# A new order table for a hand-ordered attention and mixer program, and alpha2 of the first batch as a scale at the PSUM copies

## The chip, the cores and the metric

The kernel runs on one core of a Trainium2 chip. The metric is device time in microseconds (us), lower is better; the time of a kernel is the median of its runs. A profile shows one execution: TensorE (PE; its weight loads are PEld), VectorE (DVE), ScalarE (ACT), GpSimd (POOL), SyncE (SP) and the DMA queues.

## The reference

Block-sparse attention over 4 batches of 8 heads with 768 positions of 64 elements, followed by a mixer MLP over the 512 columns of all heads together:

```python
scores = q @ k.T / sqrt(64)                # per batch and head, 768 x 768
mask: |block_i - block_j| <= 1, first and last block row and column, 3 drawn blocks per block row (32 wide)
attn = softmax(where(mask, scores, -1e9))
x = attn @ v                               # heads side by side: [4, 768, 512]
a1 = alpha1 * x + beta1
u  = x + lam * (w_tok @ a1)                # over the 768 positions
a2 = alpha2 * u + beta2
out = u + lam * (relu(a2 @ w_ch1) @ w_ch2) # 512 -> 2048 -> 512
```

## The kernel before

All work of the four batches lies in one program without loops at run time. A string of words, `ORDER` (some 2,000 of them), names every step in the order in which it is emitted; a loop (L848 to L852) reads it and calls the step of each word. `pin_order` (L121) then fixes on each engine the order in which its instructions were emitted, and `bank_order` (L138) makes uses of one PSUM bank follow each other. So the string is the schedule: on each engine a step that waits holds all later steps of that engine. A word is a kind and a number, for some with a PSUM bank or an engine behind a colon (`d` is DVE, `a` is ACT). Two heads are a pair; pairs are numbered 0 to 15 over the batches, four to a batch, and the numbers in words count pairs, score units (nine to a pair), thirds, halves or tiles.

- `lq`, `lk`, `lv` load a pair with a cast, by POOL's DMA queue (L403), into a pool of six buffers. From pair 7 on the load is held until a flag (`F`, a tiny write on DVE, L420) by a copy on POOL (L401). `cq`, `ck`, `cv` cast or copy the loaded tile on (`copy`, L385 ACT, L387 DVE), and with that the buffer comes free. `tq`, `tk` transpose q and k by DMA from SP (L554); the first pairs go through PE instead (`H`, `hq`, `hk`).
- `q` are the scores of one unit on PE (L585 for the first five pairs, where the mask is part of the product; L595, on 64 rows, for the others), `e` the exponential on ACT (L606), `m` the mask as a minimum on DVE (L613, from pair 5 on), `p` and `r` the values on PE (L619), `n` and `nt` the division by the sums on DVE (L653, L654).
- `a`, `b` form alpha1 * x + beta1 on DVE (L691, L697), `k` is the token mix on PE (L721; needs `b`), `x` adds it to x on DVE (L730). `u` makes the bfloat16 copy `ub` of a half of a pair's columns, and `U` transposes it into `uT`: by PE into a PSUM bank for the four pairs of batch 0 (L769), with `v` as the copy from PSUM, and by a DMA transpose on SP for pairs 4 to 15 (L763).
- `f` is one 128 x 384 tile of the first channel product on PE (L787, four matmuls over the four pairs of the batch, the last of them on the pair transposed last), `g` the relu on ACT or DVE (L801, L803), `h` a quarter of an output tile of the second product on PE (L821, four matmuls), `o` the final addition on DVE (L831), `s` the write of the output on SP (L840).
- alpha2: for batch 0 `u` multiplies by `a2_bc`, a 128 x 512 tile that a broadcast load (`lc3`, 256 KB) fills. After batch 0's `f` words the eight `P` words scale `w1b` itself by `a2T` (alpha2 as 128 x 4, load `lc5`; L750 ACT, L752 DVE), and later batches use plain casts in `u`.
- `lt`, `lw`, `lx`, `lc` load weights and parameters, `z` are matmuls without a use, at the start.

Of the kernel before, what the change touches and what calls it, by code (L numbers as in the profile page):

```python
# [47 lines left out]
q1:2 e1 lv0 lk1 lq1 q0:3 lt1 cq0 hm0 z352:0 H1:2 lq2 lk2 q2:0 q3:2 e0 hq1:d hk1:d e3 q4:1 cv0:d lv1
lt0 q6:3 p0:4 e4 p1 z480:5 z128:5 q8:1 ck1:d e2 lt2 lq3 z480:5 z352:5 q5:0 p2 e6 cq1:d lk3 p3 e5 lc1
p4 q7:3 H2:5 n0 e7 r4:0 r5 r6 lc0 lc2 hk2:d H3:1 hq2:d e8 W3:4 hk3:d q9:3 lc5 r7 hq3:d q12:1 cq2:d  # L50
e9 ck2:d w3:d lv2 lq4 W2:1 r8 e12 q11:3 cv1:d H4:5 lk4 e11 n1 q10:1 p9:4 hk4:d hq4:d H5:0 e10 q16:3
hq5:d W0:5 e16 q15:1 lc3 p10 w0:d hk5:d w2:d F21 e15 lc4 lk5 p11 q13:3 W1:0 e13 q14:1 W5:5 e14 p12
# [10 lines left out]
f30:4 g9:d g30:d S5 f28:2 tk5 g28:a g29:a n8 N0 f7:3 f24:7 f0:4 f4:1 f27:2 g7:d f22:5 ck7:a f26:0
f5:3 g6:d g4:d g24:d g0:a F26 F27 g5:a F28 lv8 S1 S2 f25:1 lq9 f2:4 f23:3 f16:6 g25:d g22:a lk9 g2:d
ck8:d g23:a g26:a f3:5 O0 g16:d r40:1 g3:d lv6 r41 g27:a cq8:a tk8 r42 tk6 r43 q47:3 S0 q48:1 e47
r44 f19:0 n9 e48 f1:5 g19:d q53:3 g1:a q51:0 q52:1 f21:4 a4 e51 b4 g21:a e52 f20:5 f18:0 g20:d k9:1
f17:5 m51 m47 e53 g18:a tq6 cv7:a x9 m53 m52 g17:a k8:3 tq8 q50:0 tk7 e50 q45:3 q49:2 x8 p51:2 p52
m48 p53 e49 e45 cq9:a P7:a nt17 h0:1 F29 m49 m50 h1 F30 cv6:a F31 h2 p48:6 p49 p50 h3 lv9 lq10 lk10
nt16 q46:3 q59:2 F32 q58:1 e46 ck9:d h8:0 o0 m45 lv10 s0 tq9 m46 e59 u9:a e58 F33 m59 F34 lq11 h9
p45:6 u8:a p46 p47 h4:1 nt15 tq7 q62:1 q56:3 q61:2 a5 h10 h5 h11 e62 F35 F36 m62 m58 e56 e61 m56  # L70
q57:2 q55:1 q60:3 cv8:d lk11 o2 cq11:d b5 e57 h6 lv11 e60 ck10:d m57 lq12 P4:d h7 e55 p57:5 p58 o1
p59 U4 q70:3 q54:1 q69:0 cq10:a F37 nt19 s1 m60 e70 h20:4 lk12 tk9 s2 m61 e54 e69 m70 k10:6 p60:5
m55 p61 p62 tk10 q64:0 q66:1 F38 x10 q76:3 nt20 m69 e64 e76 h21 k11:5 m54 e66 p54:6 ck12:d cq12:a
p55 p56 x11 nt18 F39 cv9:d lv12 h22 u11:a q67:3 q65:1 q68:0 e65 h23 h24:5 p69:2 lq13 a6 m64 F40 e68
u10:a lk13 b6 m66 F41 m68 k12:3 e67 ck11:a p70 q71:0 e71 q63:3 h25 m65 x12 o5 m67 lv13 p66:4 e63 m71
k13:1 m63 x13 p67 u13:a p71 tk11 p68 U5 nt23 nt22 p63:7 p64 u12:a P6:a p65 h26 nt21 F42 a7 b7 h27 U6
tq10 q78:1 q74:0 q72:3 e78 k14:4 o6 x14 e74 k15:5 x15 m78 u14:d u15:a e72 s5 h16:1 h17 P5:d m74 U7
P0:d ck13:d h18 lq14 cv10:d F43 q80:2 q75:1 q81:3 tq11 e75 lk14 m72 h19 e81 f46:0 f44:2 P1:a f47:3
# [5 lines left out]
g58:a e85 m89 g55:d a8 b8 m83 f53:5 f39:0 f32:4 f35:1 g53:a g39:a m82 g35:d g62:d g32:a f50:7 g50:d
f60:2 g60:a f57:3 m85 f61:4 g57:a q87:0 q93:3 g61:a q84:1 e84 k17:5 p81:4 e93 k16:2 e87 x17 m84
f63:6 x16 p84:3 m87 g63:a p82 p85 p86 nt28 p83 p87:5 nt27 q92:3 q98:0 q88:1 h36:4 tk12 s6 u17:d e92
m92 e88 e98 h37 h38 m88 s4 m98 p88 p89 h39 nt29 a9 b9 m91 o9 m93 q90:1 q94:3 q95:0 e95 h32:5 e94 e90
m90 m95 h33 h34 m94 q96:3 q100:0 q105:1 tq12 s9 e96 k18:4 h35 tq13 m96 p93:6 o8 x18 cv12:d p90:7
e100 e105 p94 p91 p92 q97:0 nt30 q110:1 q107:2 e97 p95 k19:7 nt31 e107 m97 p96:6 tk14 e110 x19
q103:0 q102:2 m107 u16:a p97 p98 u19:d nt32 u18:d e103 m105 a10 U8 h40:2 h41 tk13 U9 e102 m102 h42  # L90
q101:3 q104:0 p105:4 h43 e101 p102:3 b10 e104 m101 k21:5 m103 m104 p103 o10 q99:0 q106:3 ck15:a e99
s8 p104 h52:2 s10 e106 x21 m100 m99 k20:5 m106 p99:0 p100 nt34 p101 p106 p107 h48:3 m110 nt33 nt35
x20 h53 a11 q118:3 b11 q108:0 e118 q111:2 h49 e108 u20:a k22:6 u21:d k23:7 x22 U10 h50 cq15:d x23
e111 h54 h51 h55 q114:2 u22:a u23:d U11 tq14 o13 f75:0 f72:6 f74:7 f78:1 f73:2 e114 f67:5 tk15 g72:d
# [6 lines left out]
p115 g83:d m117 g91:a p124 f80:3 p116 g82:a cv15:d p125 nt38 p117:5 h64:4 g80:d nt41 p118 h65 a12
q133:3 q119:0 q122:1 e119 b12 cv14:d h66 e133 h67 m119 e122 p119 o16 h68:0 nt39 q121:3 q130:1 q120:2
m122 k25:1 h69 e120 m120 e121 k24:4 e130 m121 p120:7 x24 p121 p122 x25 h70 nt40 h71 a13 b13 q131:2
q128:3 q126:1 e131 e126 e128 u24:a k26:1 h88:4 x26 m131 o17 u25:d k27:5 q129:3 q136:1 m126 q140:0
x27 U12 h89 e129 h90 u27:d m129 s17 s16 m130 m128 e140 e136 h91 q127:0 q134:1 o22 e127 q132:3 p129:5
m133 p130 s22 p131 e134 m127 h84:0 nt43 p126:1 p127 p128 m134 q135:1 e132 q142:2 q138:3 e135 m132
nt42 h85 e142 e138 p132:2 m135 m136 p133 p134 h86 u26:a nt44 a14 q137:1 q141:2 b14 e137 e141 q143:3
h80:1 p135:2 h87 m142 m137 e143 m141 p136 p137 p141:3 p142 q139:3 k28:4 k29:5 e139 m140 nt45 m143
m138 p143 x28 m139 p138:2 p139 x29 p140 h81 nt47 u29:a u28:a nt46 h82 U14 a15 h72:6 b15 U13 o21
k31:4 k30:7 x31 u31:d h83 h73 x30 u30:d h74 o20 U15 s21 h75 f110:3 f98:4 f99:2 f103:1 f105:5 f112:7  # L110
f126:0 o18 g112:d g105:a s18 s20 f124:5 f106:6 g126:d f101:0 g103:d g99:d f97:7 g101:d f116:2 f109:1
# [79 lines left out]
def kernel(  # L191
# [239 lines left out]
    @on("lc")  # L431
    def _(i):
        t, src = (
            (lam_bc, moe_lam), (a1_bc, moe_alpha1), (b1_bc, moe_beta1), (a2_bc, moe_alpha2), (be2T, moe_beta2),
            (a2T, moe_alpha2),
        )[i]
# [298 lines left out]
        if p not in ub:  # L735
            ub[p] = wk.tile([P, NT, P], BF, name="ub", tag="ub", bufs=2)
        dst, src = ub[p][:, 3 * g : 3 * g + 3, :], x_of(p, 3 * g, 3, 0, P)
        if p >= NPAIR:
            copy(eng, dst, src)
        else:  # L740
            nc.vector.tensor_tensor(out=dst, in0=src, in1=per_col(a2_bc, p, 3, 0, P), op=ALU.mult)

# [25 lines left out]

    @on("v")
# [112 lines left out]
```

## Time and profile before

| | before |
|---|---|
| median of 3 runs | 309.06 us (308.7 to 309.21) |
| the profiled execution, its own time | 308.34 us |
| its span | 306.6 us |
| busy PE / DVE / ACT / POOL | 298.3 / 219.4 / 199.7 / 53.0 us |
| granted TensorE clock | 1.00 |
| moved by DMA | 31.18 MB, mean 102 GB/s |

A line of the timeline or of the groups gives the line of the kernel, the engine, the operation with the names of what it writes and reads, shapes, and a count. In the timeline the first two numbers are start and length in us, and a bracket gives the idle time ahead of it on its engine and what ended that; neighbouring instructions of one kind are one line. In the groups stand busy time in us and the mean length of one in ns, then idle time. The windows give a stretch, its length, and the busy time of PE, PEld, DVE, ACT and POOL in it with counts, then the clock, the DMA share and GB/s. DMA issues list KB and the median us from issue to landing. Times of neighbours on one engine overlap by a little, so what one instruction costs in a full queue is the distance from start to start.

### The profile page before, as it was taken

Reading aid. Unit: us, or ns where it says so; the run is one execution under the profiler, and the core shown is the slowest. Engines: PE = TensorE matmul, PEld = TensorE weight load, DVE = VectorE, ACT = ScalarE, POOL = GpSimd, SP = SyncE. Lnnn points to the kernel's source line nnn. Section 1 sums busy time; section 2 is a strip of 40 time slices with the busy share of each in tenths; the row PEclk is TensorE's granted clock in tenths of the full one; section 3 lists DMA queues with packets and bytes.
Section 4 is the critical chain, followed back from the end, with each engine's and each line's share of the span. In section 5 each row is a group of like instructions: output and inputs, shape, how many; then the busy total and the mean of one; then the engine's idle time right before and its main releaser. Section 6 shows DMA issues by size and latency. Waiting matters only on the chain.

```text
span 306.6 us, 7765 instructions
## 1 busy us (share of the span) xinstructions
PE 298.3 (97%) x3301; PEld 192.4 (63%) x3301; DVE 219.4 (72%) x473; ACT 199.7 (65%) x264; POOL 53.0 (17%) x95
## 2 busy tenths in 40 slices
PE   8999999999999899899999999999999999999995
PEld 4677888666755576475757665656666675565443
DVE  4599989587779798587788994746968997452112
ACT  4999998848989785889858844277376851134100
POOL 5546651231234231132000000000000000000000
PEclk9999999999999999999999999999999999999999
DMA  6999999959699899665002515301000303300022
GB/s 154 181 249 205 199 207 207 195 116 182 129 157 172 160 95 149 80 148 77 3 2 62 135 38 105 95 0 36 2 2 15 116 3 63 119 2 0 0 105 103
DMA packets 48399, 31.18 MB, mean 102 GB/s; under 512 B 29020, under 2 KB 44140, under 8 KB 48364
## 3 DMA queue, kind: packets, MB, share of 16 engines
q0 software_dynamic: 16016, 15.47, 32.3%
q1 hardware_dynamic: 32132, 14.97, 21.7%
q8 instruction: 26, 0.43, 0.5%
q10 hardware_dynamic: 216, 0.24, 0.2%
q14 instruction: 9, 0.07, 0.1%
HBM read 31.45 MB, written 6.88 MB: 125 GB/s over the span
## 4 chain that ended last, share of the span: by engine, by line
PE 76%; DVE 11%; DMA 5%; ACT 4%; issue 2%; POOL 1%; SPq 0%; ACTq 0%; DVEq 0%; POOLq 0%
PE psum L787 27%; PE psum L821 20%; PE psum L721 9%; PE psum L619 8%; PE psum L595 6%; ACT eT L606 3%; PE psum L585 3%; DMA uT<-ub 2%; DMA k<-in_k_dram 2%; DVE eT L613 2%; PE psum L299 1%; DVE x_sb L730 1%; DVE x_sb L654 1%; DVE kx L387 1%; DVE qx L387 1%
## 5 line engine op out<-in xcount | busy, mean ns | idle before, releaser
L606 ACT ACTIVATE eT<-psum 128x1024 f16<-128x1024 f32 x145 | 138.3, 1021 | 37.4 <-PE psum L595 34.1
L821 PE MATMUL psum<-w2b,hts 128*128 128x512 bf16 (+1 forms) x400 | 90.4, 371 | 0.0
L787 PE MATMUL psum<-uT,w1b 128*128 128x384 bf16 (+1 forms) x512 | 87.1, 326 | 1.4 <-DMA uT<-ub 1.3
L613 DVE TENSOR_TENSOR eT<-eT,maskT 128x1024 f16<-128x1024 f16 x99 | 64.9, 686 | 9.2 <-ACT eT L606 9.0
L787 PEld LDWEIGHTS <-w1b 128*128 128x128 bf16 x512 | 48.8, 98 | 35.7 <-ACT eT L606 2.3
L801 ACT ACTIVATE hts<-psum,b1t 128x384 bf16<-128x384 f32 x70 | 37.6, 585 | 35.0 <-PE psum L787 34.5
L821 PEld LDWEIGHTS <-hts 128*128 128x128 bf16 x400 | 36.3, 98 | 37.6 <-issue 3.2
L803 DVE TENSOR_SCALAR hts<-psum,b1t 128x384 bf16<-128x384 f32 x58 | 34.3, 615 | 27.2 <-PE psum L787 26.6
L619 PEld LDWEIGHTS <-eT 128*128 128x128 f16 x1152 | 42.8, 97 | 9.1 <-issue 1.5
L619 PE MATMUL psum<-vext,eT 128*128 128x65 f16 x1152 | 46.6, 193 | 0.4 <-DVE eT L613 0.3
L721 PE MATMUL psum<-a1p,wtokT 128*128 128x128 bf16 x576 | 36.8, 219 | 0.2
L721 PEld LDWEIGHTS <-wtokT 128*128 128x128 bf16 x576 | 33.5, 98 | 4.3 <-issue 1.4
L831 DVE TENSOR_TENSOR ot<-x_sb,psum 128x512 f32<-128x512 f32 (+1 forms) x25 | 16.6, 662 | 19.8 <-PE psum L821 14.1
L595 PE MATMUL psum<-qx,kx 64*128 64x256 bf16 x396 | 27.9, 271 | 0.9 <-DVE flag L420 0.9
L585 PE MATMUL psum<-qx,kx 88*128 88x512 bf16 (+1 forms) x120 | 25.8, 326 | 0.4 <-DVE kx L387 0.3
L595 PEld LDWEIGHTS <-kx 64*128 64x128 bf16 x396 | 16.3, 94 | 11.9 <-issue 4.6
L730 DVE TENSOR_TENSOR x_sb<-x_sb,psum 128x384 f32<-128x384 f32 x32 | 17.5, 549 | 7.8 <-PE psum L721 7.6
L401 POOL COPY held<-flag 1x1 bf16<-1x1 bf16 x27 | 8.9, 331 | 38.5 <-DVE flag L420 38.4
L691 DVE TENSOR_TENSOR a1p<-x_sb,a_bc 128x768 bf16<-128x768 f32 (+1 forms) x17 | 15.3, 905 | 0.2
L654 DVE TENSOR_TENSOR x_sb<-psum,rcp 128x256 f32<-128x256 f32 x33 | 14.0, 424 | 1.1
L403 POOL DMA_DIRECT2D q<-in_q_dram x15 | 10.7, 715 | 19.4 <-DVE flag L420 6.4
L403 POOL DMA_DIRECT2D v<-in_v_dram x16 | 11.6, 725 | 14.2 <-DVE rel L387 5.8
(70 smaller groups left out, 163.1 us busy)
## 6 DMA issues: line engine op xcount, KB each, us to landing
out_dram<-ot SPq DMA_DIRECT2D x23, 256.0 KB, 2.9
v<-in_v_dram POOLq DMA_DIRECT2D x16, 192.0 KB, 6.6
k<-in_k_dram POOLq DMA_DIRECT2D x15, 192.0 KB, 5.7
q<-in_q_dram POOLq DMA_DIRECT2D x15, 192.0 KB, 6.1
w2b<-in_moe_w_ch_dram POOLq DMA_DIRECT2D x4, 512.0 KB, 13.4
w1b<-in_moe_w_ch_dram POOLq DMA_DIRECT2D x4, 512.0 KB, 8.8
wtk<-in_moe_w_tok_dram POOLq DMA_DIRECT2D x3, 384.0 KB, 10.3
mask_rows<-maskT SPq DMA_DIRECT2D x1, 576.0 KB
```

The lines of the kernel that those rows point to most:

```text
L403: nc.gpsimd.dma_start(t[:], pair_ap(src, *batch(p)))
L585: nc.tensor.matmul(t[:, f : f + w], kx[h][0:KC, ts(jt, P)], qx[h][0:KC, c : c + w], start=True, stop=True,)
L595: nc.tensor.matmul(t[:, (2 * a + j) * TH : (2 * a + j + 1) * TH], kx[h][r, ts(2 * g + j, P)], qx[h][r, ts(th, TH)], start=True, stop=True,)
L606: nc.scalar.activation(eTs[n][:, c], t[:, c], AF.Exp, bias=EXPB, scale=SCALE)
L613: nc.vector.tensor_tensor(out=e, in0=e, in1=mask, op=ALU.min)
L619: nc.tensor.matmul(ops[key][:, t * VW : t * VW + D + 1], eTs[n][:, c : c + P], vext[n // NU % NV][:, a, jt, 0 : D + 1], start=(first and z ...
L721: nc.tensor.matmul(t[:, j, :], wtokT[:, s, ts(3 * g + j, P)], a1p[p][:, s, :], start=(s == 0), stop=(s == NT - 1),)
L730: nc.vector.tensor_tensor(out=sl, in0=sl, in1=tps.pop(i), op=ALU.add)
L787: nc.tensor.matmul(hps[i][:, 0:w], w1b[:, dk, ts(f, P)], uT[b][:, dk, hf * HS : hf * HS + w], start=(dk == 0), stop=(dk == 3),)
L801: nc.scalar.activation(hts[kk][:, f, :], t[:, 0:HS], AF.Relu, bias=b1t[:, f : f + 1], scale=1.0)
L803: nc.vector.tensor_scalar(out=hts[kk][:, f, :], in0=t[:, 0:HS], scalar1=b1t[:, f : f + 1], scalar2=0.0, op0=ALU.add, op1=ALU.max,)
L821: nc.tensor.matmul(cps[i][:, 0:w], hts[kk][:, nk, ts(m, P)], w2s[0][:, nk, lo : lo + w], start=(nk == 0), stop=(nk == 15),)
```

## The change

The whole table is a new one, found by a search in which more time passes until transposes and loads count as landed. Beside it alpha2 of batch 0 moves: `u` is a plain cast for all pairs, `v` multiplies by `a2T` while it copies out of PSUM, and the load of `a2_bc` (`lc3`) is gone from the table. In the code:

```diff
     @on("lc")
-            (lam_bc, moe_lam), (a1_bc, moe_alpha1), (b1_bc, moe_beta1), (a2_bc, moe_alpha2), (be2T, moe_beta2),
+            (lam_bc, moe_lam), (a1_bc, moe_alpha1), (b1_bc, moe_beta1), None, (be2T, moe_beta2),
...
     @on("u")
-        if p >= NPAIR:
-            copy(eng, dst, src)
-        else:
-            nc.vector.tensor_tensor(out=dst, in0=src, in1=per_col(a2_bc, p, 3, 0, P), op=ALU.mult)
+        copy(eng, dst, src)
...
     @on("v")
     def _(p, eng):
-        copy(eng, mixed(p), ups.pop(p).rearrange("p o c -> p (o c)"))
+        t, a2 = ups.pop(p).rearrange("p o c -> p (o c)"), a2T[:, p : p + 1]
+        if eng == "a":
+            nc.scalar.mul(mixed(p), t, a2)
+        else:
+            nc.vector.tensor_scalar(out=mixed(p), in0=t, scalar1=a2, scalar2=None, op0=ALU.mult)
```

The tables have the same steps but for `lc3` and the `z` words (five before, three after); `v0`, `v1`, `v2`, `v3` stand on ACT, ACT, DVE, DVE before and on DVE, ACT, ACT, DVE after. The stretches that the prediction speaks of, first the loads and casts of pairs 11 and 12 up to `k14`, then `k14` to the first `f` of batch 1, then pair 15 near the end (only the words that matter here, in their order):

```diff
-o0 ... lq11 ... lk11 o2 cq11:d b5 ... ck10:d m57 lq12 P4:d ... cq10:a ... lk12 ... k10 ... k11 ... m54 e66 p54 ck12:d cq12:a ... lk13 ... k12 ... ck11:a ... k13 ... b7 ... k14
+o0 ... lq11 ... h11 cq11:d P6:d o2 ... lk11 ... ck10:a ... lq12 ... ck11:d P1:d x11 ... lk12 ... cq12:d ... cq10:d ... k10 ... k12 ... k13 ... lk13 ck12:a ... b7 ... k14
...
-k14 o6 x14 e74 k15 x15 m78 u14:d u15:a e72 s5 h16 h17 P5:d m74 U7 P0:d ck13:d h18 ... q80 q75 q81 ... h19 e81 f46 f44
+k14 k15 u13:a x14 e74 e79 u14:d h16 U6 q80 q77 q72 s6 x15 u15:d e80 U7 F43 m76 ck13:d e72 h17 h18 P2:d tk10 h19 m80 e77 P5:d lq14 q75 q78 q73 f44
...
-a15 h72 b15 U13 o21 k31 k30 x31 u31:d h83 h73 x30 u30:d h74 o20 U15 s21 h75 f110
+a15 b15 h73 h74 x29 k31 u29:a x28 o21 k30 x31 x30 h80 u28:a h75 u31:a u30:d s21 h81 U14 U15 h82 h83 o18 f98
```

`v0` to `v3` and `lc5` at the start:

```diff
-lc5 r7 hq3:d ... U0 ... v0:a ... U1 ... v1:a ... U2 ... S3 B0 v2:d U3 p37 e42 p38 v3:d q43 p39 ... f15
+lc5 lk6 hk7:d ... U0 lw2 e27 q34 k3 hk8:a v0:d ... U1 ... v1:a ... U2 q42 u6:d v2:a U3 e43 p37 S6 v3:d p38 p39 p40 f15
```

More of the change, by code (lines that the diff above doesn't have):

```diff
@@ L47 @@
 ORDER = """
[L48 to L52, printed above, removed]
@@ L63 @@
[L63 to L67, printed above, removed]
@@ L68 @@
[L68 to L78, printed above, removed]
@@ L84 @@
[L84 to L94, printed above, removed]
@@ L101 @@
[L101 to L111, printed above, removed]
@@ new lines @@
+r16 hk6:d q18:2 e20 L1 e17 L0 a0 e18 q24:3 q23:0 r17 b0 e24 hq7:d F22 cv2:d n3 k1:4 q26:3 k0:5 x1
+cq4:d lv3 lc5 lk6 hk7:d e23 q21:0 p18:4 q28:1 e26 lx1 e21 e28 x0 q29:3 r22:5 p19 r23 q31:0 r24 r25
+cq6:d r26 a1 F23 ck4:d lv6 ck5:d u1:d u0:d lw0 lq7 lw3 lc4 lw1 e29 b1 cv4:d n5 q30:1 p20 p21 H9:7
+e31 p22 H8:6 q27:0 e30 n4 hq9:d cv3:d hk9:d U0:5 lw2 e27 q34:1 k3:4 hk8:a v0:d e34 lx2 p27:7 q33:0
+lq5 x3 e33 hq8:d F24 p28 q32:2 a2 k2:6 q35:1 e32 p29 b2 u3:d q37:0 ck6:d F25 x2 q44:2 u2:d p30 r31:6
@@ new lines @@
+m45 m56 nt16 q58:2 h8:0 h9 P0:a e58 h4:2 h5 h10 F35 P4:d m58 h11 cq11:d P6:d o2 p45:3 lk11 p46 s0
+ck10:a p47 cv8:d nt15 F36 h6 lv11 a5 q57:2 q62:3 q61:0 b5 e57 h7 e61 k11:4 e62 m57 lq12 p57:5 q60:0
+o1 ck11:d P1:d x11 m62 q55:1 F37 e60 s1 q70:3 p58 p59 lk12 nt19 m61 F38 m60 h20:4 cq12:d e55 h21 m55
+cq10:d F39 e70 q66:1 q54:0 lv12 tq10 U4 u11:a q69:3 s2 e54 k10:5 e66 m54 e69 x10 p60:0 p61 p62 h22
+lq13 nt20 q76:1 q65:0 q64:3 p54:5 e76 p55 p56 m66 m70 h23 F40 e65 e64 m69 nt18 F41 a6 b6 o5 m65
+q68:0 q63:1 h24:5 F42 u10:a k12:6 p69:7 p70 e68 q67:0 e63 x12 m63 q71:1 s5 h25 p63:6 p66:4 e71 m64
@@ new lines @@
+m68 tq11 tk11 k13:3 m71 e67 p71 p64 cv9:a lk13 ck12:a u12:a m67 U5 x13 p65 p67 nt23 p68 lv13 nt21
+h26 nt22 a7 b7 h27 q81:3 q74:0 e81 q79:1 o6 k14:4 k15:5 u13:a x14 e74 e79 u14:d h16:4 U6 q80:0 q77:1
+q72:3 s6 x15 u15:d e80 U7 F43 m76 ck13:d e72 h17 h18 P2:d tk10 h19 m80 e77 P5:d lq14 q75:1 q78:3
+q73:0 f44:5 cv10:a P3:d F44 o4 e75 e78 m74 e73 g44:d m78 lk14 f46:4 f36:3 cq13:d f45:7 f47:6 f37:2
+lv14 g36:a m81 m72 f38:5 f39:3 m77 g47:d g38:a f48:0 g46:a g45:a g37:a f42:5 f41:6 f34:1 g39:d m73
+f56:7 f52:2 f59:3 g42:a f62:4 f33:5 g56:a F45 cq14:d g52:a g41:d g59:a g48:a ck14:a m79 F46 g34:a
@@ new lines @@
+m75 lq15 lk15 g33:d g62:d f43:6 g43:a f49:0 p75:1 g49:a p76 p77 p78:6 nt25 p79 p80 q86:1 q89:0 q91:2
+nt26 e86 f40:7 f51:6 f58:2 f57:3 e89 e91 g58:d g57:d f61:5 f54:4 g40:a g51:a g54:a g61:d m86 p72:6
+p73 p74 q82:1 q83:0 q85:2 nt24 f50:7 f35:6 m91 e83 e85 e82 f63:1 g50:d m83 f32:0 p81:5 f53:2 g63:a
+a8 g35:a f55:7 f60:4 m82 g32:d b8 g53:a p82 cv11:d g55:a m85 g60:a q84:3 q87:0 e84 q93:1 m89 k17:4
+m84 e87 x17 F47 k16:6 p84:7 p85 m87 x16 p86 lv15 p83 p87:4 nt28 e93 q92:0 q88:1 e92 e88 q98:3 nt27
@@ new lines @@
+U8 e99 m106 k20:6 m99 x20 p102:7 p105:1 p99:0 U9 tq13 e101 p106 m101 x21 p107 nt35 ck15:a p100 u20:a
+p103 p101 nt33 p104 h49 nt34 h50 a11 q108:3 q111:1 q118:0 b11 e108 k23:5 k22:6 u21:d U10 x23 x22
+e118 e111 u23:a u22:d h56:5 h57 h51 s8 U11 m110 o12 cv12:a m118 tk14 h58 h59 s12 f70:6 f79:7 tk15
+f72:1 f78:2 f76:4 g78:a g79:d g72:a f77:7 f71:2 f67:3 m108 f85:0 g71:a f68:1 g77:d g70:d g67:a g76:a
+f66:6 o14 g68:d g85:d g66:a f75:4 q114:1 q113:3 q109:0 g75:d e113 f74:5 f73:4 m111 g74:d g73:a e114
@@ new lines @@
+q119:1 q133:3 nt41 m122 b12 q120:0 e119 m119 h66 e120 h67 s14 e133 p119 q130:0 q121:1 q128:3 e121
+nt39 k24:4 k25:3 h68:2 m121 m120 x24 e130 x25 u24:a p120:4 e128 p121 u25:d p122 nt40 tq15 U12 h69
+h70 h71 o16 a13 b13 o17 h88:4 q131:1 q126:0 m133 q129:3 m130 s17 k26:5 e126 k27:0 e129 e131 x26 m126
+x27 m131 m129 m128 h89 q127:3 q136:0 q140:1 e127 p126:5 h90 p129:7 e140 e136 m127 u26:a p130 p131
+h91 q134:0 nt43 u27:a e134 q132:3 q135:1 o22 m136 p127 p128 h84:4 e132 m134 nt42 h85 e135 m132
+q137:0 q138:3 m140 m135 q142:1 e137 m137 U13 s22 h86 p132:5 p133 p134 e142 nt44 h87 a14 e138 b14
@@ new lines @@
+q141:0 q143:1 q139:3 e141 p135:5 m138 p136 p137 k29:0 m141 e143 m143 m142 k28:1 p138:2 p141:3 e139
+m139 nt45 p142 p143 p139 nt47 s16 p140 h72:7 nt46 a15 b15 h73 h74 x29 k31:2 u29:a x28 o21 k30:5 x31
+x30 h80:1 u28:a h75 u31:a u30:d s21 h81 U14 U15 h82 h83 o18 f98:3 f102:6 f105:2 f127:0 f121:5 g127:a
+f103:7 f112:4 g112:a o20 g98:d g102:a s18 g121:d f118:5 f120:3 g103:d f119:7 f114:6 g114:a g105:d
+g120:a f109:0 g118:d f108:2 f117:5 f97:4 f96:3 f123:6 g97:d g123:d f113:4 g117:a g108:a f115:1
+g109:a f124:6 f122:5 g115:a f111:2 g122:a f99:1 f100:5 g113:a g111:a f125:4 f104:0 g124:a g96:a
```

58 lines of the change are left out of this document (31 added, 27 removed).

## The prediction

> **What bounds the kernel now.** I read the busy shares and the split of the chain first, then the windows, then the order of time around each place where TensorE stands still.
>
> ```profile
> PE 298.3 (97%) x3301; PEld 192.4 (63%) x3301; DVE 219.4 (72%) x473; ACT 199.7 (65%) x264; POOL 53.0 (17%) x95
> PE 76%; DVE 11%; DMA 5%; ACT 4%; issue 2%; POOL 1%; SPq 0%; ACTq 0%; DVEq 0%; POOLq 0%
> 85.35:116.40 31.05, 29.79 (x396) 18.98 (x394) 26.93 (x66) 25.32 (x31) 10.71 (x21) 1.00 1.10 146
> 140.00:240.00 100.00, 99.94 (x1128) 63.29 (x1126) 76.31 (x148) 64.05 (x83) 1.28 (x2) 1.00 0.20 48
> ```
>
> TensorE is busy for 97% of the span at a granted clock of 1.00. A new order of the same work can only close the gaps, which are a few us in all. In the columns of the windows (length, then PE, PEld, DVE, ACT, POOL) 140 to 240 us holds nothing to win: 99.94 of 100. The other stretch, 85 to 116 us, has PE and DVE busy 29.79 and 26.93 of 31.05 us, and both queues depend on each other there: PE's scores, ACT's exponentials, DVE's mask, PE's values. Its gaps, and those right behind it and near the end, are named by the timeline and the chain:
>
> ```profile
> 93.65 1.90 PE L821 MATMUL psum<-w2b,hts 128*128 128x512 bf16 x8
> 95.84 0.91 PE L619 MATMUL psum<-vext,eT 128*128 128x65 f16 x24 [0.29 <-DVE eT L613]
> 94.06 0.36 DVE L387 COPY rel<-q 128x768 bf16<-128x768 bf16 x1 [0.32 <-DMA q<-in_q_dram]
> 103.53 1.03 PE L821 MATMUL psum<-w2b,hts 128*128 128x512 bf16 x4
> 105.44 0.83 PE L595 MATMUL psum<-qx,kx 64*128 64x256 bf16 x12 [0.89 <-DVE flag L420]
> 104.01 0.36 DVE L387 COPY rel<-k 128x768 bf16<-128x768 bf16 x1 [1.91 <-DMA k<-in_k_dram]
> 97.38 6.61 DMA k<-in_k_dram
> 122.78 0.65 PE L787 MATMUL psum<-uT,w1b 128*128 128x384 bf16 x3
> 124.72 4.87 PE L787 MATMUL psum<-uT,w1b 128*128 128x384 bf16 x29 [1.29 <-DMA uT<-ub]
> 120.34 4.34 DMA uT<-ub
> 257.56 3.62 PE L821 MATMUL psum<-w2b,hts 128*128 128x512 bf16 x16
> 261.01 4.21 PE L787 MATMUL psum<-uT,w1b 128*128 128x384 bf16 x23
> 259.02 2.74 DMA uT<-ub
> ```
>
> The 16 w2 matmuls from 257.56 to 261.01 give 3.45/4 = 0.863 us for each h word (four matmuls). With it PE's gaps follow from the starts. The first is 95.84 − 93.65 − 2 × 0.863 = 0.46 us: p57 waits for a mask that stood behind the cast cq11, which waited for its load. The second is 105.44 − 103.53 − 0.863 = 1.05 us: q67 waits for the flag behind the cast ck12, which stood 1.91 us in front of a load issued at 97.38 that took 6.61 us. The third: f44's first three matmuls start at 122.78, take 3 × 0.163 = 0.49 (4.87 less a tail of 0.15, over 29), and the fourth needs U7's transpose, so it waits 124.72 − 123.27 = 1.45 us. The last: three matmuls from 261.01, then U15 lands at 259.02 + 2.74 = 261.76: 0.3 us. Together 3.2 us, all four by a cast or matmul that meets a DMA not yet landed.
>
> **The change part by part.** Load waits. In the new table ck12 is on ACT and comes long behind lk12; cq11, ck11 and cq12 remain on DVE. So 1.5 us of PE waiting loses its cause, and what is late next is DVE itself. From o0 to b7, on which k14 waits, DVE gets by the two tables one m, one nt, two u and two P more (casts even out, two flags fewer).
>
> ```profile
> 97.34 2.49 DVE L613 TENSOR_TENSOR eT<-eT,maskT 128x1024 f16<-128x1024 f16 x4
> 118.66 0.56 DVE L730 TENSOR_TENSOR x_sb<-x_sb,psum 128x384 f32<-128x384 f32 x1 [0.45 <-PE psum L721]
> 119.13 0.68 DVE L613 TENSOR_TENSOR eT<-eT,maskT 128x1024 f16<-128x1024 f16 x1
> 119.73 0.55 DVE L387 CAST ub<-x_sb 128x384 bf16<-128x384 f32 x1
> 120.19 0.47 DVE L752 TENSOR_SCALAR w1b<-w1b,a2T 128x1024 bf16<-128x1024 bf16 x1
> 120.59 0.68 DVE L613 TENSOR_TENSOR eT<-eT,maskT 128x1024 f16<-128x1024 f16 x1
> 96.79 0.18 DVE L653 RECIPROCAL rcp<-psum 128x4 f32<-128x4 f32 x1
> 97.00 0.42 DVE L654 TENSOR_TENSOR x_sb<-psum,rcp 128x256 f32<-128x256 f32 x1
> ```
>
> From start to start: m is 0.60 (119.13 to 119.73, and (2.49 − 0.68)/3), u 0.46 (119.73 to 120.19), P 0.40, nt 0.55 (96.79 to 97.34). The addition is 0.60 + 0.55 + 2 × 0.46 + 2 × 0.40 = 2.9, less 0.1 for the flags: DVE's own work becomes 26.93 + 2.8 = 29.7 us. PE's, without its 1.5 us of load waits, is 31.05 − 1.5 = 29.6. So the cover over DVE that made the rest of its idle time free is gone: each us that DVE stands still there now moves k14. Before, DVE idled 31.05 − 26.93 = 4.1 us, of which 0.32 + 1.91 = 2.2 at loads, so 1.9 at other things (exponentials mostly). Bounds for what is left are 0 and 1.9; I take 0.9, the middle, because no row is nearer to one end. The stretch then takes 30.6 instead of 31.05: −0.45 us (−1.4 to +0.55).
>
> U7. Before, m78 (0.60) stood between x15 and u14 on DVE, and u14 ended at 120.28, after which U7 was issued at 120.34. The new table has u14 ahead of h16, and x15, u15 straight behind one another, both on DVE, then U7. From x15's start that is 0.47 + 0.55 + 0.06 + 4.34 = 5.4 us (x15 started at 118.66, right at k15's end). PE's cover from k15's end is now h16, three score words, h17 to h19, three score words and three matmuls of f44.
>
> ```profile
> 109.53 0.61 PE L595 MATMUL psum<-qx,kx 64*128 64x256 bf16 x8
> 110.08 1.04 PE L821 MATMUL psum<-w2b,hts 128*128 128x512 bf16 x4
> 121.14 0.83 PE L595 MATMUL psum<-qx,kx 64*128 64x256 bf16 x12
> 121.90 1.04 PE L821 MATMUL psum<-w2b,hts 128*128 128x512 bf16 x4
> ```
>
> Three score words take 121.90 − 121.14 = 0.76, so the cover is 4 × 0.863 + 2 × 0.76 + 0.49 = 5.5 us: as long as the chain. U6 and an output write lie ahead of U7 on SP, so I leave 0.2 (0 to 0.6): −1.25. If this cover failed wholly the old 1.45 would be back. For U15 the new table has five h words after k30 where there were four: a cover of 5 × 0.863 + 0.49 = 4.8 us from the first of them, while U15 landed 261.76 − 257.56 = 4.2 us behind that point: −0.3.
>
> Score groups. Two words take 0.55, three 0.76, so a word is 0.21 and each run of score words has a fixed 0.13. The runs (64 rows, pairs from 5 on) go from 50 to 47: −0.4 us, on PE itself.
>
> Alpha2 of batch 0. The eight multiplies of L741 become casts, and the four PSUM copies get a scale:
>
> ```profile
> L741 DVE TENSOR_TENSOR ub<-x_sb,a_bc 128x384 bf16<-128x384 f32 x8 | 4.4, 556 | 0.3
> L387 DVE CAST ub<-x_sb 128x384 bf16<-128x384 f32 x10 | 5.5, 548 | 0.2
> L385 ACT COPY uT<-psum 128x768 bf16<-128x768 bf16 x2 | 1.6, 808 | 0.3 <-PE psum L769 0.3
> L385 ACT COPY rel<-q 128x768 bf16<-128x768 bf16 x7 | 5.9, 842 | 0.0
> L606 ACT ACTIVATE eT<-psum 128x1024 f16<-128x1024 f32 x145 | 138.3, 1021 | 37.4 <-PE psum L595 34.1 <-PE psum L585 1.9 <-issue 1.2
> L750 ACT ACTIVATE w1b<-w1b,a2T 128x1024 bf16<-128x1024 bf16 x4 | 4.6, 1154 | 0.0
> 0.00:54.00 54.00, 52.13 (x731) 38.71 (x732) 43.59 (x106) 47.83 (x55) 27.79 (x47) 1.00 1.11 200
> a_bc<-in_moe_alpha_dram POOLq DMA_DIRECT2D x2, 256.0 KB, 7.3
> a2T<-in_moe_alpha_dram POOLq DMA_DIRECT2D x1, 2.0 KB, 7.9
> ```
>
> 556 against 548 ns: nothing, eight times. On ACT a scale from a pointer is bounded by its copy of the same 768 (808) and the scaled 1024 (1154): between 0 and 0.35 us each for v1 and v2. v3, on DVE, is the last before the first f word, so I cost ACT's two at nothing; without that cover they are 0.7 at most. The Trainium skill, "ScalarE: Activation LUTs", section "What ACT_TABLE_LOAD costs", says that each [128,1] pointer operand adds about 93 ns to an ACTIVATE. By it the two together cost an estimated 0.2 us, which speaks against this edit but leaves the sum as it is. The dropped load (256 KB, 7.3 us to landing) frees a place early, where PE is busy 52.13 of 54 us and waits for exponentials, not loads: 0 (−0.5 to +0.3, a gain or loss of PE's 1.9 idle us by a quarter). The four v now wait for a2T, which took 7.9 us to land; between lc5 and v0 the table has eight exponentials, 8 × 1.02 = 8.2 us on the busiest helper there, so 0 with a thin cover; if it failed, DVE would stand at v0 with batch 0's a2 and x3 behind it, up to some 1 us.
>
> Sum: 308.34 − 0.45 − 1.25 − 0.3 − 0.4, and + 0.2 for small new waits elsewhere, is 306.1. That profiled execution lay 0.72 under the median of 309.06 and has 1.7 us outside its span, which I leave alone. So 306.9 us.
>
> **The rivals.** *DVE becomes the bound (slower).* If DVE idles from o0 to b7 as long as before, 4.1 us, the stretch takes 29.7 + 4.1 = 33.8, that is 3.2 more than I counted: 310.1 us. It decides from an idle time of 3.7 us, where the total passes 309.7. For it: the own work of DVE and PE is equal, 29.7 and 29.6, and they wait for each other. Against: 2.2 of the 4.1 stood before two loads, of which the longer moves off DVE.
>
> *A load wait comes back.* cq12 or ck11 on DVE meets a load as ck12 did:
>
> ```profile
> k<-in_k_dram POOLq DMA_DIRECT2D x15, 192.0 KB, 5.7
> 93.44 0.71 POOL L403 DMA_DIRECT2D k<-in_k_dram  x1 [4.55 <-DVE vext L387]
> ```
>
> A median of 5.7 us with the old 6.61 among them, against some 5 us of DVE work between cq11 (which frees lk11's buffer) and ck11. A wait of 1.9 again gives 306.9 + 1.9 = 308.8. The Trainium skill, "DMA: Bandwidth & Descriptors", section "Anatomy of one DMA", fits 2.0 us plus bytes over 436 GB/s, an estimated 2.5 us for 192 KB. By it ck12 would never have waited and this rival would be void; the trace, 6.61 and a median of 5.7, does not agree.
>
> *The change does not do what it says.* The transposes and loads move with their readers and land as late as before; only the fewer score runs remain: 308.7 to 309.1.
>
> **How the numbers follow.** About 0.2% (0.6 us) is what a measurement here can tell from no change. Forecast 0.63, all of it faster; load wait 0.13, mostly within 0.2% (0.04 faster); no effect 0.05, and with it the rest of the load case, 0.14 same; DVE as the bound 0.19, slower. That is faster 0.67, same 0.14, slower 0.19. The best end has no idle DVE (−0.95 more), U7 and the small waits at 0 (−0.4) and the early gain of 0.5: 305.0. The worst that I hold is short of the DVE case's full price: 309.8.
>
> **What would show it.** Right: no load bracket over 0.5 on a DVE cast between 85 and 116 us, U7's f run unbroken, the window from o0 to k14 near 30.6 us with DVE over 95% busy, f in one run after U15. Wrong: PE waiting for k14 or k12 by over 2 us with DVE full or idle behind exponentials; a DVE cast in front of a load; a gap at the first f of batch 0 behind a2T; or the start (PE to 54 us) moved by over 0.5.

## The result

The changed kernel takes 307.59 us (median of 15 runs, 306.08 to 309.31) against 309.06 us (15 runs, 308.31 to 310.45): a ratio of 0.9948, with a 95% interval of 0.9927 to 0.9969. That is 1.5 us less; 2.2 had been forecast. Its profiled execution took 308.79 us with a span of 307.0, which is 1.2 us above its median and longer than that of before: the profile shows a bad draw, and why it is one is the main thing to read in it. (The table has 1,362 words before and 1,359 after, not some 2,000 as said above.)

The page of after, busy shares and the split of the chain, and the windows that answer to those of before:

```profile
PE 299.7 (98%) x3299; PEld 194.5 (63%) x3299; DVE 218.8 (71%) x474; ACT 198.6 (65%) x263; POOL 51.7 (17%) x94
PE 79%; DVE 7%; DMA 7%; ACT 4%; issue 1%; SPq 0%; DVEq 0%; ACTq 0%
86.88:118.11 31.23, 30.46 (x407) 19.15 (x404) 29.75 (x70) 23.90 (x28) 8.94 (x16) 1.00 1.09 146
140.00:240.00 100.00, 99.57 (x1156) 64.56 (x1155) 75.08 (x145) 67.55 (x87) 1.23 (x2) 1.00 0.23 46
```

The stretch from o0 to k14 is now 31.23 us long (31.10 before) and VectorE is busy for 29.75 of it, as worked out (29.7). The places at which TensorE stood still before, in the timeline of after:

```profile
103.19 0.35 DVE L387 COPY rel<-q 128x768 bf16<-128x768 bf16 x1
125.30 2.94 PE L788 MATMUL psum<-uT,w1b 128*128 128x384 bf16 x17
261.11 3.09 PE L788 MATMUL psum<-uT,w1b 128*128 128x384 bf16 x18
98.03 0.69 DVE L832 TENSOR_TENSOR ot<-x_sb,psum 128x512 f32<-128x512 f32 x1 [0.47 <-DMA out_dram<-ot]
97.02 1.17 PE L721 MATMUL psum<-a1p,wtokT 128*128 128x128 bf16 x18 [0.31 <-DVE a1p L697]
118.11 2.17 PE L721 MATMUL psum<-a1p,wtokT 128*128 128x128 bf16 x36 [0.34 <-DVE a1p L697]
186.69 2.17 PE L721 MATMUL psum<-a1p,wtokT 128*128 128x128 bf16 x36 [0.39 <-DVE a1p L697]
```

No cast stands in front of a load in this stretch any more, and f44 and f98 run on without a break behind U7 and U15. New are three waits at token mixes, k11, k14 and k23: each time on the b of that mix. By the starts (start, less the pitch of what ran before) they are 0.48, 0.41 and 0.46 us. And VectorE stands 0.47 us at o2, whose buffer is still being written out: a stop at a transfer that the prediction had not listed.

What the prediction had put at nothing is the start. The first lines are before, then after; the last is a step of after's chain:

```profile
4.58 0.85 PE L336 MATMUL psum<-identb,rel 128*128 128x128 bf16 x6
7.74 0.50 PE L336 MATMUL psum<-identb,rel 128*128 128x128 bf16 x6
53.75 4.57 PE L787 MATMUL psum<-uT,w1b 128*128 128x385 bf16 x27
```

```profile
5.14 0.80 PE L336 MATMUL psum<-identb,rel 128*128 128x128 bf16 x6 [0.35 <-DMA identb<-ident_c]
7.33 2.77 PE L585 MATMUL psum<-qx,kx 88*128 88x512 bf16 x8
9.89 0.82 PE L336 MATMUL psum<-identb,rel 128*128 128x128 bf16 x6
55.68 0.50 PE L788 MATMUL psum<-uT,w1b 128*128 128x385 bf16 x2
1.68 3.42 DMA identb<-ident_c
```

The identity table landed after the filler (the matmuls without a use at the start) had ended, TensorE paused for 0.35 us, and from there six transposes still took 0.82 us at 9.89 where before they took 0.50 at 7.74. The granted clock is given as 1.00 in both; only the lengths of single matmuls show the slow rate. The Trainium skill, "TensorE: Matmul & The Clock Gate", section "Part 1: The HAM clock gate (the "warmup" mystery)", describes such a thing: half rate until a window of some 3.4 us has been busy, at a point that varies from run to run. The trace agrees in kind: 0.82 against 0.50 us, until about 10 us. The first f word came 1.93 us later than before; from there to the end of the span after took 251.3 us and before 252.85.

### The profile page after: what moved, and what is told of

It is laid out like the page before. It is cut to its first block, busy times and chain, and to the rows that moved or that the text cites. A ratio compares the mean times of both kernels' runs of the same rounds, so it can differ in the third digit from the quotient of the medians.

```text
span 307.0 us, 7772 instructions
## 1 busy us (share of the span) xinstructions
PE 299.7 (98%) x3299; PEld 194.5 (63%) x3299; DVE 218.8 (71%) x474; ACT 198.6 (65%) x263; POOL 51.7 (17%) x94
## 4 chain that ended last, share of the span: by engine, by line
PE 79%; DVE 7%; DMA 7%; ACT 4%; issue 1%; SPq 0%; DVEq 0%; ACTq 0%
PE psum L788 27%; PE psum L822 20%; PE psum L721 10%; PE psum L619 9%; PE psum L595 6%; PE psum L585 5%; ACT eT L606 4%; DMA kx<-rel 2%; DVE eT L613 2%; DMA out_dram<-ot 2%; DMA k<-in_k_dram 2%; DVE a1p L691 1%; DMA identb<-ident_c 1%; DVE x_sb L654 1%; PE psum L336 1%
## 5 line engine op out<-in xcount | busy, mean ns | idle before, releaser
L606 ACT ACTIVATE eT<-psum 128x1024 f16<-128x1024 f32 (+1 forms) x145 | 138.0, 1022 | 32.2 <-PE psum L595 29.3
L788 PE MATMUL psum<-uT,w1b 128*128 128x384 bf16 (+1 forms) x512 | 85.4, 326 | 0.0
L802 ACT ACTIVATE hts<-psum,b1t 128x384 bf16<-128x384 f32 x73 | 38.7, 584 | 32.3 <-PE psum L788 31.7
L804 DVE TENSOR_SCALAR hts<-psum,b1t 128x384 bf16<-128x384 f32 x55 | 33.0, 615 | 28.3 <-PE psum L788 27.6
L619 PE MATMUL psum<-vext,eT 128*128 128x65 f16 x1152 | 45.9, 193 | 0.0
L721 PE MATMUL psum<-a1p,wtokT 128*128 128x128 bf16 x576 | 36.0, 219 | 1.3 <-DVE a1p L697 1.3
L585 PE MATMUL psum<-qx,kx 88*128 88x512 bf16 (+1 forms) x120 | 27.1, 340 | 0.1
L403 POOL DMA_DIRECT2D k<-in_k_dram x15 | 10.9, 728 | 36.1 <-ACT vext L385 17.4
L585 PEld LDWEIGHTS <-kx 88*128 88x128 bf16 x120 | 10.0, 101 | 5.3 <-issue 1.1
```

The lines of the kernel that those rows point to most:

```text
L403: nc.gpsimd.dma_start(t[:], pair_ap(src, *batch(p)))
L585: nc.tensor.matmul(t[:, f : f + w], kx[h][0:KC, ts(jt, P)], qx[h][0:KC, c : c + w], start=True, stop=True,)
L606: nc.scalar.activation(eTs[n][:, c], t[:, c], AF.Exp, bias=EXPB, scale=SCALE)
L619: nc.tensor.matmul(ops[key][:, t * VW : t * VW + D + 1], eTs[n][:, c : c + P], vext[n // NU % NV][:, a, jt, 0 : D + 1], start=(first and z ...
L721: nc.tensor.matmul(t[:, j, :], wtokT[:, s, ts(3 * g + j, P)], a1p[p][:, s, :], start=(s == 0), stop=(s == NT - 1),)
L788: nc.tensor.matmul(hps[i][:, 0:w], w1b[:, dk, ts(f, P)], uT[b][:, dk, hf * HS : hf * HS + w], start=(dk == 0), stop=(dk == 3),)
```

## The experiments

The table lists each profiled execution: its time, its first f word, and what its span holds from there on; beside it the median, the number of runs and the ratio to the kernel before on the same chip. The first rows are those of the comparison above.

| kernel | median (runs) | ratio, 95% interval | profiled | first f | rest of span |
|---|---|---|---|---|---|
| before | 309.06 (15) | 1 | 308.34 | 53.75 | 252.85 |
| after | 307.59 (15) | 0.9948, 0.9927 to 0.9969 | 308.79 | 55.68 | 251.3 |
| again | 306.80 (6) | 0.9935, 0.9913 to 0.9957 | 307.56 | 54.75 | 251.05 |
| after_warm | 305.87 (5) | 0.9908, 0.9892 to 0.9925 | 305.88 | 53.96 | 250.1 |
| before_warm | 308.98 (12) | 1.0011, 0.9994 to 1.0029 | 308.65 | 53.78 | 253.1 |
| before_alpha2 | 308.50 (12) | 1.0001, 0.9984 to 1.0018 | 310.10 | 55.64 | 252.7 |
| aw_dve | 306.69 (12) | 0.9947, 0.9925 to 0.9969 | 306.41 | 53.96 | 250.6 |
| aw_u7 | 308.28 (12) | 0.9993, 0.9968 to 1.0019 | 308.11 | 54.21 | 252.1 |
| aw_ck12 | 306.35 (10) | 0.9923, 0.9895 to 0.9951 | 305.73 | 53.52 | 250.4 |
| before_load | 307.65 (12) | 0.9969, 0.9947 to 0.9991 | 307.50 | 53.69 | 252.0 |
| best | 307.36 (12) | 0.9946, 0.9925 to 0.9968 | 306.80 | 54.40 | 250.6 |
| after_cold | 308.98 (12) | 1.0006, 0.9986 to 1.0027 | 309.36 | 57.44 | 250.2 |
| before_fix | 306.46 (7) | 0.9935, 0.9912 to 0.9958 | 307.64 | 53.64 | 252.3 |
| aw_noalpha | 306.33 (6) | 0.9922, 0.9905 to 0.9939 | 306.61 | 54.70 | 250.1 |

**again**: the changed kernel without an edit.

> The changed kernel without any edit, for a second profile. Theory (the start of the profiled execution was bad luck): its first matmuls waited 0.35 us for the identity table, TensorE stayed at the slow rate until about 9.9 us, and the first f word came at 55.7 us where before had 53.75; in another execution the first f word comes at 53.5 to 55 us, and from there to the end it is again 251.3 us (+-0.4). Time 307.6 (307.2 to 308.0). Rival (the new table's own start is slower by nearly 2 us): first f word at 55.5 us or later again.

In this profile the start was fast (L585 x8 in 1.47 us), and the rest of the span 251.05. But the first f word still came at 54.75:

```profile
6.38 1.47 PE L585 MATMUL psum<-qx,kx 88*128 88x512 bf16 x8 [0.33 <-DVE qx L356]
q8 instruction: 26, 0.43, 0.5%
46.60 0.89 PE L721 MATMUL psum<-a1p,wtokT 128*128 128x128 bf16 x13 [0.92 <-issue]
124.61 3.57 PE L788 MATMUL psum<-uT,w1b 128*128 128x384 bf16 x21 [0.28 <-DMA uT<-ub]
```

In the middle of k5, five matmuls in, TensorE's queue stood still for 0.92 us with no wait that the timeline names ("issue"). The DMA records offer one. Queue q8, of the kind "instruction", moves 26 transfers of 16 KB in each execution, in step with TensorE's place in its program. Here the fourth of them starts at 44.17 us, when some 1,165 of TensorE's recorded matmuls and weight loads had begun, and ends at 45.13; TensorE goes on 1.5 us later. In the twelve profiles without such a stop it starts after some 1,035 to 1,054 (at 40.65 us in after_warm). So a late load of TensorE's own instructions is the likely cause; why it was late is not shown, and no run changes it alone. And U7 landed late by 0.45 us (by the starts), so its cover is as thin as it had been worked out. The median, 306.80, lies below the range that had been expected.

**after_warm** and **before_warm**: more filler ahead of the first transposes.

```diff
-    for _ in range(4):
+    for _ in range(10):
         zero(P, 6)
```

> The changed kernel with six more 128-column filler matmuls (0.64 us at the slow rate) before the first transposes, so that TensorE has no pause there when the identity table lands late. Theory (a pause there keeps TensorE slow for some us more): full rate by 6.6 us, first f word at 54.3 us or earlier, time 306.9 (306.4 to 307.5), and a narrower spread than the 3.2 us of the changed kernel's runs. Rival (start is bound elsewhere, or the table's own start is slow): first f word at 55 us or later, time 307.6 to 308.2, as the filler only adds up to 0.6.

> The kernel before with the same six filler matmuls. Theory: its profiled execution had no pause there, so in a good execution the filler costs 0 to 0.4 us, in a bad one it saves; median 308.9 (308.4 to 309.5). Rival (filler always costs): 309.5 or more.

```profile
1.19 4.23 PE L299 MATMUL psum<-warm 128*128 128x512 bf16 x17 [1.19 <-DVE warm L296]
7.14 1.47 PE L585 MATMUL psum<-qx,kx 88*128 88x512 bf16 x8 [0.33 <-DVE qx L356]
85.20:115.69 30.49, 30.08 (x407) 19.12 (x404) 29.45 (x70) 23.87 (x28) 8.50 (x16) 1.00 0.99 149
```

No pause, full rate, first f at 53.96, and all five runs between 305.51 and 306.05: faster than expected (306.4 to 307.5). But the filler does not take away the spread: the variants below that have it too spread by up to 2.8 us (best, 305.76 to 308.59). The kernel before gains nothing by the same filler (its interval takes in 1), so with the filler in both tables the new one is 3.1 us faster by the medians and 2.8 by the two profiles. All seven profiles with the longer filler had a fast start; of the six with the original filler (before, after, again, before_alpha2, before_load, before_fix) two had the slow one. The intervals of again and after_warm overlap, so the filler's own gain is likely, not settled.

**after_cold**: the pause forced, by less filler.

```diff
-    for _ in range(7):
+    for _ in range(5):
         zero(512, 6)
```

> The changed kernel with two of the seven 512-column filler matmuls at the start left out (0.85 us), so that TensorE has a pause before its first transposes in every execution. Theory (the pause keeps TensorE at the slow rate to about 10 us, as in the changed kernel's first profile): first matmuls of L585 at about twice their length, first f word at 55.2 to 56 us, time 307.9 (ratio 0.997; 0.995 to 0.999). Rival (the slow start had another cause): first f word at 54.8 us or earlier, ratio 0.9935 or less.

```profile
4.80 0.80 PE L336 MATMUL psum<-identb,rel 128*128 128x128 bf16 x6 [0.87 <-DMA identb<-ident_c]
6.99 2.77 PE L585 MATMUL psum<-qx,kx 88*128 88x512 bf16 x8
49.41 0.77 PE L721 MATMUL psum<-a1p,wtokT 128*128 128x128 bf16 x11 [0.85 <-issue]
57.44 1.32 PE L788 MATMUL psum<-uT,w1b 128*128 128x385 bf16 x7
```

With the pause the slow start is back: 2.77 us again for L585 x8, and a median 2.2 us above that of again, more than expected (ratio 1.0006, outside the range). The edit also takes 0.85 us of work away ahead of the pause, so the two are not told apart. In this profile the stop inside k5 is there too, so 57.44 holds both. It comes seven matmuls in and not five; but two fillers are left out, and counted from the start it is the same place in TensorE's queue, behind 1,217 recorded matmuls and weight loads in both. Here too the fourth instruction transfer is late: it starts at 47.07 us, after some 1,164.

**before_alpha2**: the table before, alpha2 moved as in the change (the code edits of the change, and lc3 out of the table).

> The kernel before with only alpha2 of batch 0 changed: plain casts, the scale at the four PSUM copies, the 256 KB load gone; its table is otherwise kept. Theory (as predicted, worth nothing): 309.06 +-0.4, first f word as before. Rivals: the missing load brings later loads earlier and the start gains 0.5 (308.5); or the copies hold ACT longer or wait for a2T and it loses 0.5 (309.6).

Ratio 1.0001: worth nothing, as predicted. Its profile drew the slow start, with the kernel before's own first steps, so this is no trait of the new table. The pause there was short (the filler's row ends at 4.79, the transposes begin at 4.91), so how long a pause must be stays open. In again the same 0.12 us (4.52 to 4.64) went with a fast start; there the filler's own row had taken 3.33 us, not 3.60:

```profile
7.10 1.91 PE L585 MATMUL psum<-qx,kx 88*128 88x512 bf16 x5
55.64 3.10 PE L788 MATMUL psum<-uT,w1b 128*128 128x385 bf16 x18
```

**aw_noalpha**: after_warm with alpha2 taken back (lc3 ahead of lv4).

> The changed kernel with the six fillers and alpha2 of batch 0 as before the change: the 256 KB load is back (early, ahead of lv4), the casts multiply, the PSUM copies are plain. Theory (alpha2's move is worth nothing in this table too): ratio 0.991 (0.989 to 0.993), first f word within 0.4 us of 54.0. Rival (the missing load is what gives the start its room): first f word 0.5 us later or more, ratio 0.993 or more.

The ratio fell into the expected range; the first f word, at 54.70, is 0.3 us later than that allowed and 0.74 later than after_warm's, which was the rival's sign. TensorE waited 0.30 us ahead of U3; the other 0.45 or so had been lost before U2, and its cause stays open. The new table has u7 on ACT, and the multiply takes it to VectorE, behind u6:

```profile
52.43 1.02 DVE L741 TENSOR_TENSOR ub<-x_sb,a_bc 128x384 bf16<-128x384 f32 x2
53.51 0.51 PE L769 MATMUL psum<-identb,ub 128*128 128x128 bf16 x6
```

So in the new table the plain cast may be worth some 0.3 us, since it may go to either engine; the intervals of the two medians overlap, and it stays open.

**aw_u7**: after_warm with U7's lead taken back.

```diff
-x15 u15:d e80 U7 F43 m76 ... P5:d lq14 q75:1 q78:3 q73:0 f44:5 ... F44 o4 e75 ...
+x15 F43 m76 u15:d e80 U7 ... P5:d lq14 f44:5 ... F44 o4 q75:1 q78:3 q73:0 e75 ...
```

> The changed kernel with the six fillers, and U7's lead taken back: m76 again ahead of u15 on VectorE, and the three score words q75, q78, q73 behind f44 and f46 and not ahead of them. Theory (U7's place is what closed the gap of 1.45 us): chain 5.4 + 0.6 = 6.0 us against a cover of 4.7, so a wait of 1.3 us (1.0 to 1.7) at the fourth matmul of f44, time 307.1 (ratio 0.995). Rival (the transposes were early enough anyway, other work hides it): under 0.4 us of wait, ratio 0.992 or less.

```profile
122.26 0.65 PE L787 MATMUL psum<-uT,w1b 128*128 128x384 bf16 x3
124.35 0.32 PE L787 MATMUL psum<-uT,w1b 128*128 128x384 bf16 x1 [1.44 <-DMA uT<-ub]
```

The wait is back: 124.35 − 122.26 − 0.49 = 1.6 us, and the median 2.4 us above after_warm's. U7's place is what closed that gap. The rest of the span is 2.0 us longer than after_warm's and the loss of the median is larger than the expected 1.2; what is lost beyond the wait stays open.

**before_load**: the table before, with ck12 moved from ahead of `cq12:a` to behind `nt18` (seven words on).

> The kernel before with the cast ck12 moved on VectorE from ahead of x11 to behind nt18, so that its load has a few us more. Theory (the load wait alone cost TensorE 1 us there, and VectorE had slack): the 0.96 us gap at q67 goes, 0.1 to 0.3 come back at k12 to k14, time 0.7 less than the kernel before (ratio 0.9977; 0.9965 to 0.999). Rival (the next wait is already there): the gap moves to m64, k12 or k14 with the same length, ratio 0.9995 or more.

```profile
104.17 0.35 DVE L387 COPY rel<-k 128x768 bf16<-128x768 bf16 x1
104.36 0.83 PE L595 MATMUL psum<-qx,kx 64*128 64x256 bf16 x12
```

The cast no longer waits, nor does q67, and the ratio is 0.9969: one moved word was worth about 1 us (0.3 to 1.6 by the interval), the size of the gap.

**aw_ck12**: after_warm with ck12 brought back to VectorE behind x10.

> The changed kernel with the six fillers, and the cast ck12 back on VectorE behind x10, soon after its load's issue, where it stands in front of the load as in the kernel before. Theory (VectorE has no slack left in this stretch): it waits there 1 to 2.5 us, and TensorE's waits between k10 and k14 grow by the same amount less what they already hold (0.5): time 306.9 to 307.9 (ratio 0.994 to 0.997). Rival (VectorE has slack as before, or the load is there in time): a wait of up to 1 us of which TensorE sees under half, ratio 0.993 or less.

```profile
98.06 0.71 POOL L403 DMA_DIRECT2D k<-in_k_dram  x1 [0.31 <-issue]
100.81 0.69 DVE L613 TENSOR_TENSOR eT<-eT,maskT 128x1024 f16<-128x1024 f16 x1 [0.40 <-ACT eT L606]
101.89 0.35 DVE L387 COPY rel<-k 128x768 bf16<-128x768 bf16 x1
```

The load was there after at most 3.8 us and the cast did not wait, as the rival had it. But the run does tell whether VectorE has slack here. In after_warm and in this run alike VectorE's last stop ahead of b7 ends 47.29 us behind the first f word (at 101.25 and 100.81), and from there it runs without a break to b7. The cast now stands in this run of work and takes 0.27 us from start to start; k14 (at 115.51) comes 61.99 us behind the first f word, 0.26 more than in after_warm (61.73). Behind its last stop VectorE has no slack, as the theory said.

**aw_dve**: after_warm with P6, P1, u8 and u9 on ACT (`:d` to `:a` in those four words).

> The changed kernel with the six fillers (305.87 us, ratio 0.9908) and, from o0 to k14, less work on VectorE: the scalings P6 and P1 and the casts u8 and u9 go to ACT (1.7 us off VectorE, 3.3 us onto ACT, which was busy 24 of 31 us). Theory (VectorE's own work bounds this stretch): TensorE's waits at k11, k12 and k14 (0.25, 0.11 and 0.41 us) go, the stretch is 0.6 us shorter, time 305.2 (ratio 0.989). Rival (the waits come from the chain of exponential, mask and values, or ACT becomes late): no wait shorter in sum, ratio 0.991 or more.

```profile
85.20:116.05 30.85, 29.70 (x401) 19.06 (x404) 28.31 (x66) 26.42 (x32) 8.42 (x16) 1.00 0.97 148
101.61 0.69 DVE L613 TENSOR_TENSOR eT<-eT,maskT 128x1024 f16<-128x1024 f16 x1 [0.77 <-ACT eT L606]
100.30 0.39 PE L595 MATMUL psum<-qx,kx 64*128 64x256 bf16 x4 [0.23 <-ACT eT L606]
116.05 2.17 PE L721 MATMUL psum<-a1p,wtokT 128*128 128x128 bf16 x36 [0.34 <-DVE a1p L697]
```

VectorE has 1.1 us less to do and the stretch is 0.36 longer; k11 still waits 0.22, k14 its 0.41, and q69 now waits for an exponential that ACT has late. The theory fell in this form: VectorE's total does not bound the stretch. But the run does not show that VectorE is free there. All four moved words stand ahead of its last stop (100.86 to 101.25 in after_warm), so what they free can only lengthen the stops; and ACT, with the added work, hands over the exponential of that stop later, so it ends at 101.61. That is 0.36 later, and k14 is 0.36 later too (the first f word is at 53.96 in both). What bounds k14 is VectorE's queue from its last stop on. k14's wait was 0.40 to 0.41 us in all eight profiles of the new table other than best (below).

**best**: after_warm with x13 behind b7, x21 behind b11 (and k23 in bank 7), cv8 behind b5.

> The changed kernel with the six fillers, and three VectorE steps moved behind the b that a token mix waits for: x13 behind b7, x21 behind b11 (with k23 in bank 7, since bank 5 is then still read), cv8 behind b5. Theory (the waits at k11, k14 and k23, 0.25, 0.41 and 0.46 us in every profile of the new table, are each one additional step in the chain nt, a, b of that place): they fall to under 0.1 each, 1.0 us in all, time 304.9 (ratio 0.9875; 0.986 to 0.989). Rival (the next wait stands right behind: U6 and U7 or U10 come later by the moved step): as much again at f44, f46 or the f behind U11, ratio 0.9905 or more.

```profile
115.37 0.55 DVE L730 TENSOR_TENSOR x_sb<-x_sb,psum 128x384 f32<-128x384 f32 x1
115.97 0.39 PE L595 MATMUL psum<-qx,kx 64*128 64x256 bf16 x3 [0.53 <-DVE x_sb L730]
116.29 2.18 PE L721 MATMUL psum<-a1p,wtokT 128*128 128x128 bf16 x36
185.18 2.18 PE L721 MATMUL psum<-a1p,wtokT 128*128 128x128 bf16 x36 [0.69 <-ACT eT L606]
```

cv8's move did what was meant: k11's wait is gone. The other two did not: TensorE resumed at 115.97, when x13 ended (115.92) and not b7, and the last three score matmuls ahead of k14 were held as well, so the wait grew from 0.41 to 0.81 us, and that at k23 from 0.46 to 0.75. Both are a matter of PSUM banks, as the table and these brackets show. A unit of scores fills two of the eight banks, 1,024 columns: `q79:1` is banks 2 and 3. `k13:3` left its result in bank 3, and x13 is the step that reads it, so with x13 moved behind b7 the last three matmuls of q79 (the first of its four needs bank 2 alone) waited for it, and k14 behind them. k23 was sent to bank 7, which the scores of `q108:3` (banks 6 and 7) held until e108 had read them. With other banks b7's lead might have counted; that was not tried. Its median is no better than that of the other variants.

**before_fix**: before_load, and U7's chain tightened in the old table.

```diff
-k15:5 x15 m78 u14:d u15:a e72 s5 h16:1 h17 P5:d m74 U7 P0:d
+k15:5 u14:d x15 u15:d e72 s5 h16:1 h17 U7 m78 P5:d m74 P0:d
```

> The kernel before, its own table, with two local moves: ck12 behind nt18 (as before), and for U7 u14 ahead of x15, u15 on VectorE straight behind x15, m78 behind U7. Theory (these gaps are local): the 0.96 us gap is gone, U7 is issued 0.6 us earlier and the wait at f44 falls from 1.45 to 0.85; 1.5 us together, time ratio 0.995 (0.9935 to 0.997). Rival (what is moved comes back behind it: m78 and P5 late, so g or f late): ratio 0.998 or more.

```profile
110.29 7.36 DMA uT<-ub
117.74 0.55 DVE L386 CAST ub<-x_sb 128x384 bf16<-128x384 f32 x1 [0.72 <-DMA uT<-ub]
123.89 3.41 PE L786 MATMUL psum<-uT,w1b 128*128 128x384 bf16 x20 [1.65 <-DMA uT<-ub]
```

The median is 0.9935 of before, as expected (0.995), but this profile does not show why: u14 could not start early, as its buffer (two of them) was still read by U5's transpose, which took 7.36 us to land; so U7 left no earlier against f44's first matmuls (2.22 us ahead of them, 2.44 before) and f44 waited 1.8 us by the starts. The profiled run is among the slower of the seven (305.82 to 308.01). What the faster ones had gained beyond before_load stays open. The range overlaps that of the whole new table.

## Why the prediction was right, and where its sum was off

The time lay in the range, on the forecast side, and the main mechanism was shown from both sides. Term by term, with after_warm as the profile without a disturbed start (its rest of span is 2.7 us shorter than before's):

- **Load waits.** Right. They are gone in every profile of the new table, and the one of ck12 alone, taken away in the old table, was worth 1 us.
- **U7** was put at −1.25 and brought −1.45 in after and after_warm, −1.0 in again. Right, with the thin cover that was said. **U15**, −0.3: right, f98 to the end of its run without a break.
- **The stretch from o0 to k14** was put at −0.45: 30.49 against 31.10 in after_warm, −0.6; in after +0.1. VectorE's work was put at 29.7 us and is 29.75 and 29.45; its idle time was put at 0.9 and is 1.5 in after, 1.0 in after_warm. The step "each us that DVE stands still there now moves k14" holds for VectorE's last stop and what stands behind it: where that stop ended 0.36 us later k14 came 0.36 later (aw_dve), and 0.27 us of work added behind it moved k14 by 0.26 (aw_ck12). It does not hold for the sum over the stretch, for work taken off ahead of that stop only turned into idle time. In after k14 comes 0.7 us later behind the first f word than in after_warm; the stop of 0.47 at o2 stands in that chain, so much of the difference is likely to be its. The slower rival did not come because the idle time it needs (3.7 us) was not there.
- **Score runs** were put at −0.4, for 50 runs that become 47. Counted in the order of TensorE's own steps, runs of score words of pairs from 5 on go from 36 to 34, which at 0.13 us each is −0.26. No run takes this term by itself.
- **Small new waits** were put at +0.2 for all the rest. k23 alone is 0.46; against it stands a gain of 0.4 between 240 and 250 us that had not been seen. The two cancel. A further 0.36 us was won between the first f word and o0 (31.24 us in after_warm, 31.60 before), which no term names.
- **Alpha2**: nothing in the old table, as said. The two rows of ACT's copy give the pointer's price, which had been bounded by 0 and 0.35 us:

```profile
L772 ACT ACTIVATE uT<-psum,a2T 128x768 bf16<-128x768 bf16 x2 | 1.8, 900 | 0.2 <-PE psum L766 0.2
L774 DVE TENSOR_SCALAR uT<-psum,a2T 128x768 bf16<-128x768 bf16 x2 | 1.2, 618 | 0.1
```

  900 against 808 ns, 92 ns each. The Trainium skill, "ScalarE: Activation LUTs", section "What ACT_TABLE_LOAD costs", says about 93, and the trace agrees. v3 was the last ahead of f, so it was covered. There was no wait for a2T.
- **The start**, put at 0 (−0.5 to +0.3), is the step that was mis-sized. It cost 1.93 us in after's profile and 1.0 in again's, 0.2 in after_warm's. The new table without these is worth 2.5 us (profiled: 305.88 against 308.34), near the 2.2 of the forecast (2.8 to 3.1 against before_warm, which has the same filler); by the ratios of after and again 1.6 to 2.0 is left in the medians. Two things were seen: TensorE's slow rate behind a pause of a few tenths, which both tables can draw, and the stop in k5 (0.92 and 0.85 us), in two of the nine profiles of the new table and none of the five of the old, each time with a late load of TensorE's instructions. They are not all: in best and aw_noalpha the first f word is at 54.40 and 54.70 without either. Why the new table's medians lose more by the start than the old one's is not settled; that the stop in k5 comes on top is a guess from two profiles.
